# Sliding-window attention and a gated MLP: q and k loaded as four tokens per partition, and the first batch taken into the common loop

## The chip, the cores and the metric

The kernel runs on one core of a Trainium2 chip. The metric is device time in microseconds (us), the median of several executions. The core has five engines that run side by side and wait for one another through semaphores: TensorE (PE in the profile, with its weight loads as PEld), VectorE (DVE), ScalarE (ACT), GpSimd (POOL) and SyncE (SP). SP, ACT and POOL also start DMA transfers; SP does nothing else here. SBUF and PSUM are on-chip memories of 128 partitions; TensorE writes its results to PSUM.

## The reference

Eight batches, each with 8 heads, 576 tokens and 64 elements per head, all in float32. Attention looks back over a window of 64 tokens; the heads are then joined to 512 columns per token, and a gated MLP (gMLP) mixes along the tokens.

```python
scores = (q @ k.T) / sqrt(64)
mask = (rel >= 0) & (rel < 64)          # rel = query position - key position
attn = softmax(where(mask, scores, -1e9))
x = (attn @ v), heads joined            # 8 x 576 x 512

h = maximum(x @ w_in, 0)                # 512 -> 1024
u, v = h[..., :512], h[..., 512:]
v_n = (v - mean(v)) / sqrt(var(v) + 1e-6)
v_s = einsum('ts,bsd->btd', w_spatial, v_n) + b_spatial[None, :, None]
out = (u * v_s) @ w_out                 # 8 x 576 x 512
```

`w_spatial` is 576 x 576: it mixes all tokens of a batch, and `b_spatial` has one value per token.

## The kernel before

**Layout.** The 576 tokens of a batch are 512 plus 64: four chunks of 128 and a remainder. q, k and v come in as float32 (`NAT`, two sets of buffers, so batches i and i+2 share one), and are cast to float16 (`F16`, two sets). In the chunk layout partition p of chunk c holds token 128c + p, so every run of a load is one token of one head: 64 floats, 256 bytes. `hs` is a copy of v shifted by 64 tokens (`shift_pair`, `shift_half`), so that any 128 neighbouring keys that begin at a multiple of 64 stand in one tile.

**Attention of one batch, five steps.** Steps 0 to 3 each take two heads over the first 512 tokens, step 4 takes the remainder of all heads. `emit_T` transposes k and q of two heads on PE (eight transposes into one PSUM tile `tp`, of which there is one) and copies the tile to `qk` with one DVE copy (L216). `emit_S` multiplies each block of 64 keys with the 128 queries that may see it (16 small matmuls, into the one `sc`). `emit_E` takes the exponential on ACT and masks it with a minimum on DVE. `emit_P` computes the softmax's denominators (two matmuls with `onesK`) and the weighted sum of v (16 matmuls), into the one `oz`. `emit_N1` and `emit_N2` form the reciprocal as exp(-ln z) on ACT and multiply on DVE: the result X is a transposed x, float16.

**gMLP of one batch, units.** V (5 units; matmuls, ReLU on ACT, statistics on DVE), LN (two small ACT operations, five DVE operations that write `vn`), U (5), G (5; the spatial matmuls over `wspT`, then a DVE product) and O (5; matmuls with w_out, an ACT copy into `ob`, which has three buffers, and an output DMA). All matmul results of these units share three PSUM tiles (`mm`). `emit_W` transposes w_spatial on PE into `wspT` once; the bias lies in its row 64 of the last tile.

**Order.** Nothing is scheduled by a planner: every engine executes its instructions in the order in which the program writes them. A stage i of the main loop (from i = 2) interleaves the attention of batch i with V, LN, U, G of batch i-1 and O of batch i-2. In `att_step` the order within a step is: transposes of the next step, two units, S, P of the step before, then E, N1, N2 with one unit after each, then the units left. In stage i the loads of batch i+1 are issued on SP (L76), and POOL casts them in the same stage (L88). The kernel's last stages, 8 and 9, hold the gMLP of batch 7 and its O.

**The opening.** Batch 0 is loaded and attended pair by pair, two heads at a time: `load_by_pairs` issues 27 transfers, of which four of v are on ACT's queue and the others on SP's. `casts_step` casts k on ACT, q on DVE, v on POOL for one pair just before its transposes. Between these steps 51 matmuls on a zero tile (`warm`) run on PE. The weights are loaded and cast by DMAs that POOL issues after pairs 2 and 3 and after the remainder. Batch 1 is loaded on SP in the same pairwise form. When batch 0's attention is done, PE does V of batch 0, the five `emit_W`, LN and three U; then batch 1's attention follows with the rest of gMLP 0, its O included, between its steps (L486 to L489). The outputs of batches 0 and 1 go out on ACT's queue, the later ones on SP's (L407). Batch 2 is loaded by chunks on SP before batch 1's first transpose group is written.

Of the kernel before, what the change touches and what calls it, by code (L numbers as in the profile page):

```python
# [13 lines left out]
B = 8  # L14
# [5 lines left out]
def kernel(  # L20
# [44 lines left out]

    def load_heads(b, x, h0, eng):
        for h in (h0, h0 + 1):
            eng.dma_start(NAT[b][x][:, 0:4, h, :],  # L68
                          SRC[x][b, h, 0:512, :].rearrange("(c p) d -> p c d", p=128))
# [38 lines left out]
    scratch = cpool.tile([128, 512], f16, name="scratch")  # L108
    nc.vector.memset(scratch[:], 0.0)  # L109

    def warm(n):
        t = psp.tile([128, 512], f32, tag="mm", bufs=3, name=f"warm{nc.next_id()}")
        for _ in range(n):
            nc.tensor.matmul(t[:, :], scratch[:, 0:128], scratch[:, :], start=True, stop=True)  # L114

    def load_by_pairs(b):
        new_batch(b)
        for p in range(4):
            for x in (1, 0, 2):
                load_heads(b, x, 2 * p, nc.scalar if (b == 0 and p < 2 and x == 2) else nc.sync)  # L120
        for x in (1, 0, 2):
            load_rem(b, x, nc.sync)

    load_by_pairs(0)
    new_half(0)
    warm(16)
# [16 lines left out]
    mask = cpool.tile([128, 2, 8, 64], f16, name="mask")  # L143
    maskr = cpool.tile([128, 8, 64], f16, name="maskr")
    for h in (0, 1):
        for u in range(8):
            if u % 2 == 1:
                nc.vector.tensor_copy(mask[:, h, u, :], keep[:])
            else:
                nc.vector.tensor_scalar(mask[:, h, u, :], keep[:], -1.0, BIG, ALU.mult, ALU.add)  # L150
        nc.vector.memset(mask[64:128, h, 0, :], 0.0)
    for u in range(8):
        nc.vector.tensor_copy(maskr[:, u, :], mask[:, 0, 2, :])
# [8 lines left out]
    def casts_step(b, s, engk, engq):  # L162
        if s < 4:
            cast_pair(b, 1, s, engk)
            cast_pair(b, 0, s, engq)
            cast_pair(b, 2, s, nc.gpsimd)
            shift_pair(b, s, nc.gpsimd)
        else:
            for x in (1, 0, 2):
                cast_rem(b, x, nc.gpsimd)  # L170
            shift_rem(b, nc.gpsimd)

    class _Act:
        @staticmethod
        def tensor_copy(o, i):
            nc.scalar.copy(o, i)  # L176


    w_in_sb = [cpool.tile([128, 1024], f16, name=f"win{r}") for r in range(4)]
    w_out_sb = [cpool.tile([128, 512], f16, name=f"wout{r}") for r in range(4)]  # L180
# [383 lines left out]
```

## Time and profile before

| | |
|---|---|
| Time, median of 3 runs | 251.05 us (249.46 to 251.18) |
| The profiled execution's own time | 251.05 us |
| Its span, first to last instruction | 249.3 us |
| Mean granted TensorE clock | 0.962 |
| PE busy | 227.3 us, 91% |
| DVE busy | 155.3 us, 62% |
| ACT busy | 152.2 us, 61% |
| POOL busy | 122.1 us, 49% |
| DMA | 120,014 packets, 40.41 MB, 162 GB/s; 113,776 packets under 512 B |

A row of the profile names the source line, the engine, the operation, what it writes and reads with the number of partitions and elements, how often, its duration, and the idle time of the engine in front of it with what ended that. In rows in order of time the first number is the start in us from the span's start, the second the duration. In the slices a digit is the busy share of a fortieth of the span, in tenths. In a row of windows the columns are the stretch, its length, then the busy time of PE, PEld, DVE, ACT and POOL, the granted clock, the DMA engines' share (above 1 where queues overlap) and GB/s. Matmuls overlap in the pipeline, so the distance from one start to the next says more of PE than a duration does. The rows of a DMA queue give its packets, MB and the share of sixteen engines' span that its packets took: q1 is SP's queue, q10 ACT's, q0 POOL's.

### The profile page before, as it was taken

The page shows a single profiled execution, that of the slowest core. Times are in us where ns is not written, and L with a number is a line of the kernel's source. Part 1 is how long each engine was busy: PE and PEld are TensorE (multiplying, and loading weights), DVE is VectorE, ACT ScalarE, POOL GpSimd, SP SyncE. Part 2 cuts the span into 40 slices and gives each one's busy share as a digit, 9 for nine tenths or more (in the row PEclk, how much of TensorE's full clock was granted, in tenths as well). Part 3 has the DMA queues.
Part 4 walks back from the last instruction along what each step waited for, and adds up shares of the span by engine and source line. Part 5 has one row for each costly group of instructions (what it writes and reads, how often), then busy time and mean ns, then how long its engine had stood idle before and what let it go on. Part 6 is the DMA issues. An engine that isn't in the chain of part 4 may idle for free.

```text
span 249.3 us, 6391 instructions
## 1 busy us (share of the span) xinstructions
PE 227.3 (91%) x2588; PEld 116.8 (47%) x2588; DVE 155.3 (62%) x317; ACT 152.2 (61%) x266; POOL 122.1 (49%) x183
## 2 busy tenths in 40 slices
PE   7784996996399999999999999999999999999893
PEld 3442453553254464436544554455445544553351
DVE  6453277562459782887479556966597659755630
ACT  3373484446447666766785577756776677767423
POOL 3469638875499695369016592469135900000000
PEclk9999799799569999999999999999999999999998
DMA  8999999999999996992389948995499040014005
GB/s 159 218 184 208 216 204 229 191 201 276 249 199 210 198 178 175 246 206 52 128 192 211 192 128 221 189 198 135 137 216 156 27 165 5 3 42 149 0 3 189
DMA packets 120014, 40.41 MB, mean 162 GB/s; under 512 B 113776, under 2 KB 114864, under 8 KB 119984
## 3 DMA queue, kind: packets, MB, share of 16 engines
q1 hardware_dynamic: 114720, 34.88, 70.1%
q0 software_dynamic: 1840, 2.24, 5.2%
q10 hardware_dynamic: 3424, 2.88, 4.1%
q8 instruction: 20, 0.33, 0.6%
q14 instruction: 10, 0.08, 0.1%
HBM read 32.79 MB, written 9.44 MB: 169 GB/s over the span
## 4 chain that ended last, share of the span: by engine, by line
PE 60%; DVE 13%; ACT 9%; DMA 8%; SPq 3%; POOL 2%; issue 2%; ACTq 1%; POOLq 0%
SPq L68 3%; DMA nv_80<-in_v_dram 2%; DMA out_dram<-ob_0_1033 2%; DMA out_dram<-ob_1_3433 2%; DMA nq_78<-in_q_dram 2%; ACTq L407 1%; PE ps_0_804 L382 1%; PE warm_583 L114 1%; PE pv_0_1308 L330 1%; PE ps_0_4590 L382 1%; PE ps_0_4237 L382 1%; DVE mv_172 L336 1%; PE ps_0_3720 L382 1%; PE ps_1_895 L382 0%; PE ps_3_4653 L382 0%
## 5 line engine op out<-in xcount | busy, mean ns | idle before, releaser
L88 POOL CAST hq_2281<-nq_2285 128x512 f16<-128x512 f32 (+1 forms) x5 | 3.2, 635 | 12.8 <-DMA nq_2285<-in_q_dram 12.8
L114 PEld LDWEIGHTS <-scratch 128*128 128x128 f16 x51 | 5.0, 112 | 7.3 <-issue 3.8
L88 POOL CAST hq_3389<-nq_3393 128x512 f16<-128x512 f32 (+1 forms) x5 | 3.9, 797 | 8.8 <-DMA nq_3393<-in_q_dram 8.8
L281 PEld LDWEIGHTS <-onesK 128*64 128x64 f16 x80 | 4.6, 107 | 7.5 <-issue 5.2
L88 POOL CAST hq_2835<-nq_2839 128x512 f16<-128x512 f32 (+1 forms) x5 | 3.6, 720 | 8.3 <-DMA nq_2839<-in_q_dram 8.3
L176 ACT CAST hk_109<-nk_79 128x512 f16<-128x512 f32 x4 | 2.5, 618 | 7.5 <-DMA nk_79<-in_k_dram 7.5
L114 PE MATMUL warm_113<-scratch 128*128 128x512 f16 x16 | 5.5, 524 | 1.3 <-DVE scratch L109 1.3
L81 POOL CAST hv_110<-nv_80 128x512 f16<-128x512 f32 x4 | 2.5, 632 | 8.3 <-DMA nv_80<-in_v_dram 7.3
L88 POOL CAST hv_1729<-nv_1733 128x512 f16<-128x512 f32 (+1 forms) x5 | 3.5, 708 | 4.4 <-DMA nv_1733<-in_v_dram 4.4
L88 POOL CAST hq_1727<-nq_1731 128x512 f16<-128x512 f32 (+1 forms) x5 | 2.9, 609 | 4.6 <-DMA nq_1731<-in_q_dram 4.6
L88 POOL CAST hv_2283<-nv_2287 128x512 f16<-128x512 f32 (+1 forms) x5 | 3.2, 637 | 3.8 <-DMA nv_2287<-in_v_dram 3.8
L81 POOL CAST hv_433<-nv_437 128x512 f16<-128x512 f32 x4 | 2.5, 613 | 5.2 <-DMA nv_437<-in_v_dram 5.1
L88 POOL CAST hv_1184<-nv_764 128x512 f16<-128x512 f32 (+1 forms) x5 | 3.1, 611 | 3.9 <-DMA nv_764<-in_v_dram 3.9
L362 PEld LDWEIGHTS <-win_181 128*128 128x128 f16 x32 | 3.1, 98 | 3.8
L362 PEld LDWEIGHTS <-win_182 128*128 128x128 f16 x32 | 3.1, 98 | 3.8
L88 POOL CAST hv_1220<-nv_1224 128x512 f16<-128x512 f32 (+1 forms) x5 | 3.9, 780 | 2.0 <-DMA nv_1224<-in_v_dram 2.0
L88 POOL CAST hq_1182<-nq_762 128x512 f16<-128x512 f32 (+1 forms) x5 | 3.3, 654 | 3.2 <-DMA nq_762<-in_q_dram 2.7
L81 DVE CAST hq_108<-nq_78 128x512 f16<-128x512 f32 x4 | 1.7, 432 | 4.8 <-DMA nq_78<-in_q_dram 4.8
L281 PE MATMUL oz_3_1153<-e_1_3_1108,onesK 128*64 128x512 f16 x2 | 0.6, 611 | 4.4 <-DVE x_2_1133 L308 4.4
L88 POOL CAST hv_3391<-nv_3395 128x512 f16<-128x512 f32 (+1 forms) x5 | 3.0, 611 | 2.8 <-DMA nv_3395<-in_v_dram 2.8
L88 POOL CAST hv_2837<-nv_2841 128x512 f16<-128x512 f32 (+1 forms) x5 | 3.3, 666 | 2.0 <-DMA nv_2841<-in_v_dram 1.8
L264 ACT ACTIVATE e_1_0_831<-sc_0_813 128x1024 f16<-128x1024 f32 x1 | 1.0, 1023 | 5.2 <-PE sc_0_813 L242 5.2
(1871 smaller groups left out, 940.3 us busy)
## 6 DMA issues: line engine op xcount, KB each, us to landing
nk_79<-in_k_dram SPq DMA_DIRECT2D x9, 128.0 KB, 3.9
nq_78<-in_q_dram SPq DMA_DIRECT2D x9, 128.0 KB, 4.1
nk_436<-in_k_dram SPq DMA_DIRECT2D x9, 128.0 KB, 4.8
nq_435<-in_q_dram SPq DMA_DIRECT2D x9, 128.0 KB, 4.8
nv_437<-in_v_dram SPq DMA_DIRECT2D x9, 128.0 KB, 4.1
nk_763<-in_k_dram SPq DMA_DIRECT2D x4, 256.0 KB, 5.5
nq_762<-in_q_dram SPq DMA_DIRECT2D x4, 256.0 KB, 5.7
nv_764<-in_v_dram SPq DMA_DIRECT2D x4, 256.0 KB, 6.0
```

What stands on the lines that cost most here:

```text
L68: eng.dma_start(NAT[b][x][:, 0:4, h, :], SRC[x][b, h, 0:512, :].rearrange("(c p) d -> p c d", p=128))
L81: eng.tensor_copy(F16[b][x][:, 0:4, hs, :], NAT[b][x][:, 0:4, hs, :])
L88: eng.tensor_copy(F16[b][x][0:sn, c, :, :], NAT[b][x][0:sn, c, :, :])
L114: nc.tensor.matmul(t[:, :], scratch[:, 0:128], scratch[:, :], start=True, stop=True)
L176: nc.scalar.copy(o, i)
L264: nc.scalar.activation(e2[:, :, :], sc[:, :, :], AF.Exp, bias=0.0, scale=0.125)
L281: nc.tensor.matmul(oz[64 * h:64 * h + 64, 1, 0:n], onesK[:, :], e2[:, h, 0:n], start=True, stop=True)
L330: nc.tensor.matmul(pv[0:jn, :], xcol(b, r, j), w_in_sb[r][:, 512:1024], start=(r == 0), stop=(r == 3))
L336: nc.vector.bn_aggr(mv_t[b % NSB][0:jn, j, :], st6[0:jn, 0:6])
L362: nc.tensor.matmul(pu[:, :], w_in_sb[r][:, 128 * m:128 * m + 128], X[b, r][:, :], start=(r == 0), stop=(r == 3))
L382: nc.tensor.matmul(ps[:, :], VN[b, kk][0:kn, 128 * m:128 * m + 128], wspT[kk][0:kn, 0:512], start=(kk == 0), stop=(kk == 4))
L407: (nc.scalar if b < 2 else nc.sync).dma_start(out[b, 128 * j:128 * j + jn, :], ob[0:jn, :])
```

## The change

q and k of the first 512 tokens are loaded in another order: partition p holds tokens 4p to 4p+3 of a head, which lie side by side in memory, so a run is 1 KB (`load_pairs4`). v and the remainders stay in 256-byte runs. `cast_pair4` casts one head at a time into the old shape of `F16`, whose chunk index is now j, the token's place among the four. After the transposes column 128j + p of q and k stands for token 4p + j. Keys are put back in token order when the k half of `tp` is copied to `qk`; queries stay in the new order through S, the mask, P, X and the whole gMLP. Therefore S and P address the queries of a block as four runs (32 or 16 columns each), w_spatial is loaded and transposed in the same order, the bias row is reordered by an ACT copy, and each output DMA writes rows 4p + j.

The special opening goes. Batch 0's loads stay pairwise, now with all of v on ACT's queue; its k is cast on POOL, its q on DVE, all in front of the loop; the warm matmuls go. All weight DMAs stand on POOL after batch 0's casts and before batch 1's. The common loop now starts at i = 0: stage 0 is attention 0 with the five W at its end, stage 1 attention 1 with V, LN, U, G of batch 0, stage 2 has O of batch 0. The loads of batch i+2 are written in stage i (in stage 0 those of batches 1 and 2), three per step, in front of the step's units; the casts of batch i+1 stay in stage i. All outputs go on SP's queue.

```diff
+    def load_pairs4(b, x, h0, n, eng):
+        eng.dma_start(NAT[b][x][:, 0:4, :, :].rearrange("p j h d -> p (j h d)")
+                      .rearrange("p (h e) -> p h e", h=8)[:, h0:h0 + n, :],
+                      SRC[x][b, h0:h0 + n, 0:512, :].rearrange("h (p j) d -> p h (j d)", j=4))
+    def cast_pair4(b, x, p, eng):
+        src = NAT[b][x][:, 0:4, :, :].rearrange("p j h d -> p (j h d)") \
+            .rearrange("p (h j d) -> p h j d", h=8, j=4)
+        for h in (2 * p, 2 * p + 1):
+            eng.tensor_copy(F16[b][x][:, 0:4, h, :], src[:, h, :, :])
...
-    load_by_pairs(0)
+    new_batch(0)
     new_half(0)
-    warm(16)
+    for p in range(4):
+        for x in (1, 0):
+            load_pairs4(0, x, 2 * p, 2, nc.sync)
+        load_heads(0, 2, 2 * p, nc.scalar)
+    for x in (1, 0, 2):
+        load_rem(0, x, nc.sync if x != 2 else nc.scalar)
...
+    for p in range(4):
+        cast_pair4(0, 1, p, nc.gpsimd)
+        cast_pair4(0, 0, p, nc.vector)
+        cast_pair(0, 2, p, nc.gpsimd)
+        shift_pair(0, p, nc.gpsimd)
+    for x in (1, 0, 2):
+        cast_rem(0, x, nc.gpsimd)
+    shift_rem(0, nc.gpsimd)
...
+        nc.gpsimd.dma_start(t[:], moe_w_in[128 * r:128 * (r + 1), :])
+    nc.gpsimd.dma_start(wq[:], moe_w_spatial[0:512, :].rearrange("(p j) s -> p j s", j=4))
+    nc.gpsimd.dma_start(wr[:], moe_w_spatial[512:576, :])
+    nc.gpsimd.dma_start(brow[64:65, :], moe_b_spatial[:].unsqueeze(0))
+        nc.gpsimd.dma_start(t[:], moe_w_out[128 * r:128 * (r + 1), :])
...
-                nc.vector.tensor_copy(qk[:, :], tp[:, :])
+                nc.vector.tensor_copy(qk[:, 512:1024].rearrange("d (p j) -> d p j", j=4),
+                                      tp[:, 512:1024].rearrange("d (j p) -> d p j", j=4))
+                nc.vector.tensor_copy(qk[:, 0:512], tp[:, 0:512])
...
-                        nc.tensor.matmul(sc[r:r + 64, h, c0:c1],
-                                         qk[d, 512 + 64 * kap:576 + 64 * kap], qk[d, c0:c1],
+                        nc.tensor.matmul(sc[r:r + 64, h, :].rearrange("k (j p) -> k j p", j=4)[:, :, p0:p1],
+                                         qk[d, 512 + 64 * kap:576 + 64 * kap], q4[d, :, p0:p1],
                                          start=True, stop=True)
...
+                    if s < 4:
+                        o_ = o_.rearrange("k (j p) -> k j p", j=4)[:, :, 16 * u:16 * u + 16]
+                        e_ = e_.rearrange("k (j p) -> k j p", j=4)[:, :, 16 * u:16 * u + 16]
...
-        (nc.scalar if b < 2 else nc.sync).dma_start(out[b, 128 * j:128 * j + jn, :], ob[0:jn, :])
+        dst = out[b, 0:512, :].rearrange("(p j) d -> p j d", j=4)[:, j, :] if j < 4 else out[b, 512:576, :]
+        nc.sync.dma_start(dst, ob[0:jn, :])
...
         nc.scalar.copy(wspT[kk][0:sn, 0:576], wps[0:sn, 0:576])
+        if kk == 4:
+            nc.scalar.copy(wspT[4][64:65, 0:512].rearrange("r (j p) -> r j p", j=4),
+                           brow[64:65, 0:512].rearrange("r (p j) -> r j p", j=4))
+            nc.scalar.copy(wspT[4][64:65, 512:576], brow[64:65, 512:576])
...
+    def load_list(b):
+        fs = []
+        for x in (1, 0):
+            def first(x=x):
+                if b not in NAT:
+                    new_batch(b)
+                load_pairs4(b, x, 0, 4, nc.sync)
+            fs += [first, lambda x=x: load_pairs4(b, x, 4, 4, nc.sync),
+                   lambda x=x: load_rem(b, x, nc.sync)]
+        return fs + [lambda c=c: load_chunk(b, 2, c) for c in range(5)]
...
+    emit_T(0, 0)
+    for i in range(B + 2):
+        st = units(i)
...
+        if i == 0:
+            new_batch(1)
+            loads += load_list(1)
+        if i + 2 < B:
+            loads += load_list(i + 2)
         if i + 1 < B:
             new_half(i + 1)
-            for x in (1, 0, 2):
-                casts += [lambda x=x, c=c: cast_chunk(i + 1, x, c, nc.gpsimd) for c in range(5)]
+            for x in (1, 0):
+                casts += [lambda x=x, p=p: cast_pair4(i + 1, x, p, nc.gpsimd) for p in range(4)]
+                casts += [lambda x=x: cast_rem(i + 1, x, nc.gpsimd)]
+            casts += [lambda c=c: cast_chunk(i + 1, 2, c, nc.gpsimd) for c in range(5)]
             casts += [lambda hf=hf: shift_half(i + 1, hf, nc.gpsimd) for hf in range(3)]
+        nl = (len(loads) + 4) // 5
+        ncst = (len(casts) + 3) // 4
...
-                nxt = None
-            if i < B or s == 0:
-                att_step(i, s, st[s], 2, 1, nxt)
-            run_units(st[s], 99)
+                emit_T(*nxt)
+            for _ in range(2 if i else 0):
+                if todo:
+                    todo.pop(0)()
...
```

`units(i)` returns the unit lists of a stage as the old loop wrote them (O of i-2 in step 0, V of i-1 in step 1, LN, U and G in steps 2 to 4), and in stage 0 the five W in step 4. The order within a step is that of `att_step`.

## The prediction

> **What bounds the kernel now.** I read the page's slices first, then 2 us windows for the DMA rate, then ACT, PE, DVE and POOL in order of time.
>
> ```profile
> PE   7784996996399999999999999999999999999893
> PEclk9999799799569999999999999999999999999998
> DMA  8999999999999996992389948995499040014005
> ```
>
> A slice is 6.2 us. From 69 us on PE is full, from 75 us its clock is whole: the middle and the end are bound by TensorE. Before that the DMA engines are full and PE has holes, the largest in the slice at 62 us. So a change to loading and to the first batches is priced before 92 us; from there only what lengthens or shortens a TensorE-bound stage counts.
>
> The start of T(i,1), the second transpose group of stage i, marks the stages:
>
> ```profile
> 92.10 0.39 PE L210 MATMUL tp_1_1744<-id_130,hk_1219 128*128 128x128 f16 x4
> ...
> 118.28 0.39 PE L210 MATMUL tp_1_2298<-id_130,hk_1728 128*128 128x128 f16 x4
> ```
>
> Stage 3 begins at 92.1, stage 4 at 118.3, stage 5 at 144.4: 26.1 us each. Stages 3 to 9 have the same unit order in both kernels. If the new stage 2, whose units are also those of stages 3 to 7 (O, V, LN, U, G), has its T(2,1) at t, the end is 249.3 - (92.1 - 26.1) + t = **t + 183.3**, but for what the stages themselves gain or lose. All of the question is t.
>
> The hole at 62 us shows the mechanism to watch (ACT, then PE, in order of time):
>
> ```profile
> 55.58 0.39 ACTq L407 DMA_DIRECT2D out_dram<-ob_0_1033  x1
> ...
> 60.55 0.58 ACT L406 COPY ob_3_1117<-po_3_1111 128x512 f32<-128x512 f32 x1 [0.92 <-DMA out_dram<-ob_0_1033]
> ```
> ```profile
> 64.64 0.64 PE L281 MATMUL oz_3_1153<-e_1_3_1108,onesK 128*64 128x512 f16 x2 [4.36 <-DVE x_2_1133 L308]
> ```
>
> ob has three buffers, so ob_3 waits until the output of ob_0 has landed (4.9 us among the loads, 2.0 when the queue is empty); ACT is held, and PE loses 4.4 us behind it. That was on ACT's own DMA queue.
>
> **Part 1, the DMA stream.** In pure 256-byte loads the rate is flat:
>
> ```profile
> 4.00:6.00 2.00, 2.00 (x9) 0.75 (x6) 1.66 (x12) 0.62 (x1) 0.65 (x2) 1.00 1.39 218
> 6.00:8.00 2.00, 1.43 (x12) 0.73 (x10) 0.61 (x3) 0.00 (x0) 1.18 (x2) 1.00 1.39 218
> ```
>
> 218 GB/s is 16 x 256 B / 218 = 18.8 ns per packet and engine. A batch is 13,824 such packets (3.54 MB), 16.2 us. After the change q and k are 2,048 packets of 1 KB, with 1,024 of 256 B for the remainders and 4,608 for v. No load here has 1 KB runs. Its price lies between 18.8 ns (a packet costs the same) and 75 ns (four times the bytes). From the queue rows
>
> ```profile
> q1 hardware_dynamic: 114720, 34.88, 70.1%
> q0 software_dynamic: 1840, 2.24, 5.2%
> q10 hardware_dynamic: 3424, 2.88, 4.1%
> ```
>
> q10 is 2,048 v packets and 1,376 of about 1.7 KB: 85 ns each in busy time, where q1's small ones take 22.9. A line through the two gives 55 ns for 1 KB, and scaled by 18.8/22.9 about 48 ns, which I take. A batch is then (2,048 x 48 + 5,632 x 18.8)/16 = **12.8 us**, 3.4 less.
>
> The Trainium skill ("DMA: Bandwidth & Descriptors", Specifications) gives about 27 GiB/s per engine and line rate from 512 B up, so 35 ns for 1 KB as an estimate; a batch would be 11.1 us, the first output below some 8 us earlier, and the sum 245.6.
>
> The loads also move. Before, batch 2 was issued from 44.6 us on; now SP holds batches 1 and 2 in stage 0, batch 3 in stage 1 and k of batch 4 at the head of stage 2, all ahead of the five outputs of batch 0, which change from ACT's queue to SP's. SP runs ahead as far as buffers allow: the casts that free batch 1's and 2's inputs are over early (below), so the stream never pauses, and the first output stands at its end: 2 (first bytes) + 4 x 12.8 + weights 10.3 (2.24 MB at 218) + k of batch 4 3.7 = 67 us. The same sum for the kernel before (2 + 3 x 16.2 + 10.3 + 5.4 of outputs = 66.3) stands against a last landing of batch 2 at 68.4, so I add 6% for pauses: 71, and 2.0 for landing: **73 us**. With the packet's two bounds: 55 to 89.
>
> **Part 2, the opening on POOL and PE.** The casts of k of batch 0 go from ACT to POOL, all its q casts stand ahead of the first qk copy on DVE (q of pair 3 lands after eight 256 KB transfers of 0.77 us and seven of v of 0.60, at 12.3, so attention starts at about 13 us, not 8), ACT issues nine v loads ahead of its first exponential (four took 3.13 us, so 7 us, over by then), the 51 warm matmuls go, and gMLP 0 moves from between batches 0 and 1 into stage 1. POOL now decides, since T(1,0) stands on PE ahead of S(0,4) and waits for k and q of batch 1:
>
> ```profile
> 68.41 0.61 POOL L88 CAST hv_1184<-nv_764 64x512 f16<-64x512 f32 x1 [0.43 <-DMA nv_764<-in_v_dram]
> 68.97 1.03 POOL L103 COPY hs_1185<-hv_1184 64x1024 f16<-64x1024 f16 x1
> 70.06 1.04 POOL L104 COPY hs_1185<-hv_1184 64x1024 f16<-64x1024 f16 x1
> ```
>
> 512 elements take 0.61, 1,024 take 1.04; POOL has no 256-element cast. Between 0.31 (half) and 0.61 I take 0.40, from its 128-element select (0.29). Batch 0: four pairs of 2 x 0.40 + 0.61 + 2 x 0.65 and gaps, 2.75 each from 4.5 us on, and 2.4 of remainders, 17.9; or 20.3 if v of pair 3 lands at 16. I take 19.5. Then eleven weight DMAs at 0.55, of which the last three wait for w_in to land (4.5 to 6.7 us after issue): 8, to 27.5. Then k and q of batch 1, 16 x 0.40 + 2 x 0.6 = 7.6, to 35.1; T(1,0) can start at 32. v 3.1 and four shifts 4.2: P(1,0) at **42.4** (38 to 48). ACT's chain over wspT and the two new bias copies (5.4 us from T(1,0)) ends before that. In the kernel before, P(2,0) at 74.5 to T(3,1) at 92.1 is the same work, 17.6 us; with 1.0 for a low clock after the idle opening (0.5 and 0.6 in the slices at 62 to 75 us, after the hole) t = **61.0**. Without anything else the end is 244.3.
>
> **Part 3, the stages.** k's evacuation splits from one 1,024-element copy (0.65 to 0.69) into a strided and a plain one. The plain half is qkr's row (0.40 to 0.42). A strided PSUM read is in no row: 0.42 if stride is free, 1.38 if it halves the rate of x_0's row (0.67, one element at a time); I take 0.69. Follow-on spacing makes it +0.35 per copy. Only the one in front of the five vn is near the path:
>
> ```profile
> 132.19 0.65 DVE L216 COPY qk_3_2538<-tp_3_2528 128x1024 f16<-128x1024 f16 x1
> 132.88 0.41 DVE L352 TENSOR_SCALAR vn_0_2544<-vs_0_2422,mv_172,rs_2541 128x512 f16<-128x512 f16 x1
> ...
> 133.53 0.70 DVE L352 TENSOR_SCALAR vn_2_2548<-vs_2_2485,mv_172,rs_2541 128x512 f16<-128x512 f16 x1
> ...
> 134.47 0.69 DVE L352 TENSOR_SCALAR vn_1_174<-vs_4_2513,mv_172,rs_2541 64x512 f16<-64x512 f16 x1
> ```
>
> The two long vn stand beside POOL casts. In the new kernel inputs lie ready a stage earlier and POOL's casts fall around the stage boundary, so the vn may all run at 0.33 spacing: -0.4 against +0.35. I take -0.5 in all (-3 to +7). The other copies have 0.5 us or more of DVE idleness behind them.
>
> S and P now read and write PSUM and SBUF in four runs of 16 or 32. No row has that. The 16 matmuls of S advance PE by 0.34 us and those of P by 0.35, about 22 ns each, where S streams up to 128 columns and P 64, so they seem bound by issue: I take nothing; doubled they cost 4 x 0.69 = 2.8 a stage, 19 over seven. [...]
>
> **The sum.** Profiled run: span 249.3, time 251.05 (1.75 around it), which is also the median. Opening -5.0 (66.0 to 61.0), stages -0.5: 243.8. At t = 61.0 ob_3 would be ready at 66.0 (4.96 after T, as 118.28 to 123.24); it waits for 73: +7.0, and 0.5 of clock: 251.3, time **253.0**. The 5 us won are given back at the first outputs, and 2 more.
>
> **Rivals.**
> - *The stream is ahead of the outputs* (1 KB packets below about 37 ns, or the weights' 10.3 us mostly beside the loads; it decides where output 0 lands before 66 us): 243.8 + 1.75 = 245.6. For it: 319 GB/s between 60 and 62 us where outputs mix in. Against: DMA shares of 9 tenths for 90 us.
> - *1 KB runs bring nothing*, the change doesn't do what it says: output 0 at 89, 269. Against: the queue rows.
> - *Strided matmuls cost double*, on PE in every stage from 1 on: 253 + 19 = 272. It decides from some 0.14 us per group, which over 56 groups is 8 us, more than the opening wins. For it: no row has such an access. Against: their issue-bound spacing.
>
> **Chances.** Outputs held (249 to 258) 0.47; stream ahead 0.29; packets no cheaper 0.12; strided matmuls 0.12. 80% range: 245 to 268, from the first rival to just short of the other two. One per cent is about what can be told from no change here. Faster 0.29, within 0.21 (the lower half of the forecast), slower 0.50.
>
> **What would show it.** Right: ob_3 of batch 0 waiting for the output of ob_0 for some 7 us near 70 us, a 12 to 13 us batch, PE idle from about 22 to 32 waiting for POOL, later stages near 26. Wrong: no wait at ob_3; P(1,0) away from 42; S or P groups above 0.4 us; a strided copy above 0.8.

## The result, and the profile after

The changed kernel takes **262.54 us** (median of four runs, 261.34 to 263.52). The kernel before, timed on the same chip, takes 250.25 us (249.06 to 251.18). The ratio is **1.049** (95% interval 1.041 to 1.057): slower by 4.9%, where 253.0 us was forecast. The profiled execution took 261.34 us with a span of 259.5 us, so 1.84 us lie around the span, against 1.75 before. The spans differ by 10.2 us.

The slices of the page (one is 6.5 us) and the row of SP's queue:

```profile
PE   0047149968989999999899989998999999999893
PEclk9999999997999999999999999999999999999999
DMA  7999998999877962697169805960500040005005
...
q1 hardware_dynamic: 63472, 36.58, 56.1%
```

The 1 KB runs do what they say: SP's queue moves 36.58 MB (it has all outputs now) in 63,472 packets and 56.1% of the engines' time, against 34.88 MB in 114,720 packets and 70.1%. The DMA engines are full to about 58 us, not to 90. Yet PE starts later (the digits up to 32 us are 0, 0, 4, 7, 1), and it no longer fills its slices afterwards.

PE in order of time (start, duration, then the idle time in brackets with what ended it):

```profile
33.03 0.61 PE L205 MATMUL tp_0_496<-id_102,hk_227 128*128 128x128 f16 x4 [6.27 <-POOL hk_227 L76]
36.33 0.61 PE L208 MATMUL tp_0_496<-id_102,hq_226 128*128 128x128 f16 x4 [2.69 <-POOL hq_226 L76]
...
47.99 0.42 PE L240 MATMUL sc_1_711<-qk_1_622 64*64 64x128 f16 x16
48.34 0.41 PE L279 MATMUL oz_0_729<-e_1_0_655,onesK 128*64 128x512 f16 x2
...
71.25 0.39 PE L205 MATMUL tp_1_1129<-id_102,hk_594 128*128 128x128 f16 x4
...
99.10 0.39 PE L205 MATMUL tp_1_1691<-id_102,hk_1111 128*128 128x128 f16 x4
...
126.07 0.39 PE L205 MATMUL tp_1_2253<-id_102,hk_1673 128*128 128x128 f16 x4
...
142.95 0.29 PE L216 MATMUL tp_4_2590<-id_102,hk_1673 64*128 64x64 f16 x4
...
151.84 0.41 PE L279 MATMUL oz_3_2743<-e_4_3_2657,onesK 128*64 128x512 f16 x2 [1.20 <-DVE x_2_2693 L311]
...
153.04 0.39 PE L205 MATMUL tp_1_2815<-id_102,hk_2235 128*128 128x128 f16 x4
```

The stage marks T(2,1), T(3,1), T(4,1), T(5,1) stand at 71.25, 99.10, 126.07 and 153.04. Against the aligned 66.0, 92.10, 118.28 and 144.36 of the kernel before that is 5.3, 7.0, 7.8 and 8.7 us late, and 10.2 at the end. So half of the loss is there before stage 2, and the stages add the rest: 27.8 us from the first of these marks to the second and 27.0 between the next ones, instead of 26.1. The line at 151.84 shows where in a stage: PE stands still in front of P(4,3). Its counterpart in the kernel before follows S(4,4) without a wait:

```profile
143.16 0.41 PE L281 MATMUL oz_3_2782<-e_4_3_2697,onesK 128*64 128x512 f16 x2
```

What it waits for is seen on DVE and POOL in that same stage 4 of the changed kernel:

```profile
145.44 0.69 DVE L388 TENSOR_TENSOR g_1_2617<-ps_1_2610,ru_1_2561 128x512 f16<-128x512 f32 x1 [0.73 <-PE ps_1_2610 L385]
146.86 3.72 DVE L268 TENSOR_TENSOR e_4_3_2657<-e_4_3_2657,mask 128x1024 f16<-128x1024 f16 x1 [0.72 <-ACT e_4_3_2657 L262]
...
151.11 0.68 DVE L311 TENSOR_TENSOR x_2_2693<-oz_2_2637,zi_2_2691 128x512 f16<-128x512 f32 x1
```
```profile
143.36 2.80 POOL L76 CAST hk_2797<-nk_2239 128x256 f16<-128x256 f32 x8 [8.78 <-issue]
146.12 0.61 POOL L96 CAST hk_2797<-nk_2239 64x512 f16<-64x512 f32 x1
146.68 2.81 POOL L76 CAST hq_2796<-nq_2238 128x256 f16<-128x256 f32 x8
149.43 0.61 POOL L96 CAST hq_2796<-nq_2238 64x512 f16<-64x512 f32 x1
```

The minimum that masks e of step 3 takes **3.72 us**; in the kernel before the same one took 0.69:

```profile
139.45 0.69 DVE L270 TENSOR_TENSOR e_4_3_2697<-e_4_3_2697,mask 128x1024 f16<-128x1024 f16 x1 [0.73 <-ACT e_4_3_2697 L264]
```

The long one ends at 150.58, half a microsecond after POOL's last q cast (150.04). POOL's inputs lie ready two batches ahead, so its casts of batch 6 start the moment T(4,4) (at 142.95) has read the buffer for the last time, and run 0.345 us apart without a gap for 6.7 us. The minima of step 3 in stages 2 to 5 all take 3.72 us. Behind them stand g_2 and x_2, and x_2 must free oz before P(i,3) may write it. The products from PSUM (g_1 at 145.44, 0.69 us) pass beside the same casts unhindered.

In stage 1 POOL is busy for 28.1 of 29.4 us (windows: stretch, length, busy time of PE, PEld, DVE, ACT, POOL, clock, DMA share, GB/s), and there too long instructions stand on DVE:

```profile
41.90:71.25 29.35, 25.68 (x295) 13.40 (x295) 23.24 (x38) 16.38 (x30) 28.11 (x53) 0.94 1.08 244
```
```profile
49.64 3.37 DVE L268 TENSOR_TENSOR e_1_1_749<-e_1_1_749,mask 128x1024 f16<-128x1024 f16 x1
...
66.35 2.24 DVE L268 TENSOR_TENSOR e_1_3_971<-e_1_3_971,mask 128x1024 f16<-128x1024 f16 x1 [0.73 <-ACT e_1_3_971 L262]
...
71.23 2.53 DVE L268 TENSOR_TENSOR e2r_1077<-e2r_1077,maskr 128x512 f16<-128x512 f16 x1
```

And the wait that the forecast put at 7 us is not there (SP, then ACT, in order of time):

```profile
73.37 0.36 SPq L411 DMA_DIRECT2D out_dram<-ob_0_1148  x1
```
```profile
77.09 0.58 ACT L409 COPY ob_3_1210<-po_3_1204 128x512 f32<-128x512 f32 x1
```

SP issues the first output of batch 0 right behind its copy (72.76 and 0.58), and ob_3 has no idle time in front of it.

### The profile page after: what moved, and what is told of

Read it like the earlier page. It is cut to its first block, busy times and chain, and to the rows that moved or that the text cites. A ratio compares the mean times of both kernels' runs of the same rounds, so it can differ in the third digit from the quotient of the medians.

```text
span 259.5 us, 6319 instructions
## 1 busy us (share of the span) xinstructions
PE 219.3 (85%) x2537; PEld 115.2 (44%) x2537; DVE 182.4 (70%) x352; ACT 150.8 (58%) x264; POOL 125.5 (48%) x240
## 3 DMA queue, kind: packets, MB, share of 16 engines
q1 hardware_dynamic: 63472, 36.58, 56.1%
## 4 chain that ended last, share of the span: by engine, by line
PE 54%; DVE 22%; DMA 10%; ACT 6%; POOL 4%; issue 2%; ACTq 0%
DMA nv_78<-in_v_dram 4%; DMA win_187<-in_moe_w_in_dram 4%; DVE e_5_3_3219 L268 1%; DVE e_4_3_2657 L268 1%; DVE e_2_3_1533 L268 1%; DVE e_3_3_2095 L268 1%; DVE e_1_1_749 L268 1%; DMA nk_77<-in_k_dram 1%; POOL hk_227 L76 1%; DMA out_dram<-ob_1_4667 1%; DVE e_1_3_971 L268 1%; PE ps_1_924 L385 1%; PE pu_2_916 L365 1%; PE pv_0_689 L333 1%; PE ps_0_4203 L385 1%
## 5 line engine op out<-in xcount | busy, mean ns | idle before, releaser
L279 PEld LDWEIGHTS <-onesK 128*64 128x64 f16 x80 | 5.3, 109 | 11.5 <-issue 8.9
L205 PEld LDWEIGHTS <-hk_80 128*128 128x128 f16 x16 | 1.4, 129 | 13.8 <-POOL hk_80 L76 13.0
L205 PE MATMUL tp_1_244<-id_102,hk_80 128*128 128x128 f16 x4 | 0.6, 302 | 7.8 <-DVE qk_0_220 L213 7.8
L76 POOL CAST hk_1673<-nk_1115 128x256 f16<-128x256 f32 x8 | 2.8, 394 | 8.8 <-issue 8.8
L76 POOL CAST hk_2235<-nk_1677 128x256 f16<-128x256 f32 x8 | 2.8, 394 | 8.8 <-issue 8.8
L76 POOL CAST hk_2797<-nk_2239 128x256 f16<-128x256 f32 x8 | 2.8, 394 | 8.8 <-issue 8.8
L76 POOL CAST hk_3359<-nk_2801 128x256 f16<-128x256 f32 x8 | 2.8, 394 | 8.8 <-issue 8.8
L211 DVE COPY qk_0_506<-tp_0_496 128x512 f16<-128x512 f16 x1 | 0.7, 692 | 8.2 <-PE tp_0_496 L208 8.2
L76 DVE CAST hq_79<-nq_76 128x256 f16<-128x256 f32 x8 | 2.9, 402 | 5.0 <-DMA nq_76<-in_q_dram 5.0
L266 ACT ACTIVATE e2r_547<-sc_4_509 128x512 f16<-128x512 f32 x1 | 0.6, 597 | 9.3 <-PE sc_4_509 L254 9.3
L205 PE MATMUL tp_0_496<-id_102,hk_227 128*128 128x128 f16 x4 | 0.6, 307 | 6.3 <-POOL hk_227 L76 6.3
L365 PEld LDWEIGHTS <-win_187 128*128 128x128 f16 x32 | 3.2, 99 | 3.9 <-issue 0.3
L365 PEld LDWEIGHTS <-win_189 128*128 128x128 f16 x32 | 3.2, 99 | 3.9 <-issue 0.3
L205 PE MATMUL tp_0_210<-id_102,hk_80 128*128 128x128 f16 x4 | 0.6, 308 | 4.9 <-POOL hk_80 L76 4.9
L205 PEld LDWEIGHTS <-hk_227 128*128 128x128 f16 x16 | 1.3, 122 | 7.0 <-POOL hk_227 L76 6.4
L76 POOL CAST hk_80<-nk_77 128x256 f16<-128x256 f32 x8 | 3.3, 435 | 2.2 <-DMA nk_77<-in_k_dram 2.0
L100 POOL CAST hv_3360<-nv_2802 128x512 f16<-128x512 f32 (+1 forms) x5 | 3.0, 648 | 2.5 <-PE oz_3_3305 L294 2.5
L100 POOL CAST hv_1674<-nv_1116 128x512 f16<-128x512 f32 (+1 forms) x5 | 3.0, 648 | 2.5 <-PE oz_3_1619 L294 2.5
L100 POOL CAST hv_2236<-nv_1678 128x512 f16<-128x512 f32 (+1 forms) x5 | 3.0, 648 | 2.5 <-PE oz_3_2181 L294 2.5
L100 POOL CAST hv_2798<-nv_2240 128x512 f16<-128x512 f32 (+1 forms) x5 | 3.0, 648 | 2.5 <-PE oz_3_2743 L294 2.5
L268 DVE TENSOR_TENSOR e_2_3_1533<-e_2_3_1533,mask 128x1024 f16<-128x1024 f16 x1 | 3.7, 3723 | 0.7 <-ACT e_2_3_1533 L262 0.7
## 6 DMA issues: line engine op xcount, KB each, us to landing
nk_77<-in_k_dram SPq DMA_DIRECT2D x4, 256.0 KB, 5.1
nq_76<-in_q_dram SPq DMA_DIRECT2D x4, 256.0 KB, 5.5
nv_225<-in_v_dram SPq DMA_DIRECT2D x4, 256.0 KB, 17.3
```

The costliest lines, as they stand in the source:

```text
L76: eng.tensor_copy(F16[b][x][:, 0:4, h, :], src[:, h, :, :])
L100: eng.tensor_copy(F16[b][x][0:sn, c, :, :], NAT[b][x][0:sn, c, :, :])
L205: nc.tensor.transpose(tp[:, 512 + 128 * c:640 + 128 * c], Kh[:, c, 2 * s:2 * s + 2, :], id16[:, :])
L211: nc.vector.tensor_copy(qk[:, 512:1024].rearrange("d (p j) -> d p j", j=4), tp[:, 512:1024].rearrange("d (j p) -> d p j", j=4))
L266: nc.scalar.activation(e2[:, :, :], sc[:, :, 0:256], AF.Exp, bias=0.0, scale=0.125)
L268: nc.vector.tensor_tensor(e2[:, :, :], e2[:, :, :], m, ALU.min)
```

## The experiments

**Theories.** A: POOL's unbroken rows of casts keep DVE's minima waiting, and P with them. Its two forms: any row does it (A1), or only rows of 256-element casts (A2). B: the strided copies and matmuls lengthen the stages. C: the loss is in the opening. And from the prediction: the outputs are held.

All kernels in one table. The third column is the start of x of step 3 of batch 1 on DVE (a mark that is easy to find in each trace), then the distance to the same mark of batch 2, and the distances after that up to batch 5. Each row is from that kernel's own profiled execution; the times are medians, the ratio is to the kernel before, timed beside each.

| kernel | time, ratio (95%) | mark | stage 2 | later |
|---|---|---|---|---|
| before | 250.25 | 67.0 | 25.9 | 26.2, 26.1, 26.1 |
| after | 262.54, 1.049 (1.041 to 1.057) | 74.0 | 26.3 | 27.0, 27.0, 27.0 |
| e1 POOL waits for the minimum | 259.64, 1.037 (1.032 to 1.042) | 76.5 | 25.7 | 25.7, 25.7, 25.7 |
| e2 plain copy | 262.23, 1.046 (1.037 to 1.056) | 74.3 | 26.8 | 26.8, 26.8, 26.8 |
| e3 layout alone | 261.70, 1.043 (1.036 to 1.050) | 72.7 | 27.7 | 26.2, 27.0, 27.8 |
| e4 order alone | 266.43, 1.064 (1.058 to 1.070) | 72.2 | 36.9 | 25.5, 25.5, 25.5 |
| e5 casts of 512 | 254.31, 1.013 (1.009 to 1.018) | 66.9 | 30.0 | 25.7, 25.7, 25.7 |
| e6 layout alone, casts of 512 | 258.42, 1.030 (1.026 to 1.034) | 72.2 | 25.8 | 25.8, 28.0, 25.5 |
| e7 order alone, ACT outputs | 263.80, 1.050 (1.045 to 1.055) | 72.5 | 26.4 | 27.3, 32.7, 25.5 |
| e8 casts of 512, opening by pairs | 254.88, 1.016 (1.011 to 1.022) | 61.9 | 36.8 | 25.7, 25.7, 25.7 |
| e9 as e8, ACT outputs | 250.09, 0.996 (0.993 to 1.000) | | | |
| e10 casts of 512, ACT outputs | 253.91, 1.014 (1.007 to 1.020) | 71.0 | 24.6 | 27.3, 25.7, 25.7 |
| e11 casts of 256 by tokens | 264.23, 1.055 (1.050 to 1.059) | 75.1 | 27.0 | 27.0, 27.0, 27.0 |
| e12 as e8, six ob buffers | **246.26, 0.982 (0.977 to 0.986)** | 62.1 | 25.9 | 25.7, 25.7, 25.7 |

(No marks are given for e9, whose profiled execution, 252.29 us, is the longest of its ten.)

### e1: POOL waits for the minimum

```diff
+    def pool_gap(b):
+        nc.gpsimd.tensor_copy(gapt[:, :], LASTMIN[b][0:1, 0, 0:1])   # the masked e2 of step 3
...
             for x in (1, 0):
+                if x == 0 and i > 0:
+                    casts.append(lambda i=i: pool_gap(i - 1))
                 casts += [lambda x=x, p=p: cast_pair4(i + 1, x, p, nc.gpsimd) for p in range(4)]
```

> The changed kernel with one more POOL instruction per stage: before the q casts of batch i+1 POOL copies one element of the masked e2 of step 3 of batch i-1, so it stands still until that minimum is through; nothing is left out. Theory A (POOL's unbroken row of casts, which begins when T(i,4) gives the buffer free, keeps the DVE minimum of step 3 waiting: 3.72 us against 0.69, and P of step 3 with it): the minimum of step 3 takes at most 1.2 us in stages 2 to 6, the 1.2 us PE wait in front of P(i,3) goes, stages of 27.0 become 25.3 to 26.0, and the time is 253 to 258. Theory B (strided copies and matmuls lengthen the stages): no change, 261 to 263.5. Theory C (all of the loss is in the opening and stage 1): at most 2 us less, stages still 27.0.

DVE, then POOL, in the stage at 148 us:

```profile
147.91 0.69 DVE L274 TENSOR_TENSOR e<-e,mask 128x1024 f16<-128x1024 f16 x1 [0.72 <-ACT e L268]
```
```profile
148.67 0.18 POOL L262 COPY gapt<-e 1x1 f16<-1x1 f16 x1 [0.89 <-DVE e L274]
```

With POOL standing still for 0.9 us the minimum takes 0.69 and all stages are 25.7, below the 26.1 of the kernel before. That part of A is shown: the casts, not DVE's own work, made the minimum long. B falls for the stages, as the strided copies and matmuls are all still there. The time fell by 2.9 us only, less than A expected (253 to 258 us), because stage 1 grew:

```profile
56.87 7.32 DVE L363 TENSOR_SCALAR vn<-vs,mv,rs 128x512 f16<-128x512 f16 x5
```

In stage 1, where POOL has no idle time to give, the five vn took 7.3 us beside POOL's v casts and shifts (1.7 us in a later stage, where they start 0.32 us apart). The first of them alone took 3.4 us, over a row of five casts of 512 elements. PE, left without work, ran at a granted clock of 0.5 from 58 to 69 us.

### e2: the plain copy

```diff
-                nc.vector.tensor_copy(qk[:, 512:1024].rearrange("d (p j) -> d p j", j=4),
-                                      tp[:, 512:1024].rearrange("d (j p) -> d p j", j=4))
-                nc.vector.tensor_copy(qk[:, 0:512], tp[:, 0:512])
+                nc.vector.tensor_copy(qk[:, :], tp[:, :])
```

> The changed kernel with one plain copy of 1024 columns from tp to qk as before, in place of the strided and the plain copy of 512; the keys stay in the loaded order, so the order of the keys is left out and the output is not the reference's. Theory A: DVE gets 0.41 us per step back, but the minimum of step 3 still waits for the end of POOL's row of casts (about 3.5 us): 259 to 262. Theory B: the four copies are the price of a stage, 27.0 becomes 25.5 to 26 and the time 254 to 257. Theory C: 260 to 262.

e2 leaves out the return of the keys to token order. It takes 262.23 us against 262.54, with overlapping intervals. A stage is 0.2 us shorter, and its minimum of step 3 still takes 3.72. The reordering at evacuation costs nothing that this measurement can tell.

### e3 and e4: each half of the change alone

e3 is the kernel before with the new layout. The core of its diff is the loads, the rest is as in the change:

```diff
-                load_heads(b, x, 2 * p, nc.scalar if (b == 0 and p < 2 and x == 2) else nc.sync)
+                if x == 2:
+                    load_heads(b, x, 2 * p, nc.scalar if (b == 0 and p < 2) else nc.sync)
+                else:
+                    load_pairs4(b, x, 2 * p, 2, nc.sync)
...
-            loads = [(i + 1, x, c) for x in (1, 0, 2) for c in range(5)]
+            loads = load_list(i + 1)
...
```

> The layout alone: the opening, the order and the loads' distance (batch i+1 in stage i) of the kernel before, with four tokens per partition in loads, casts, S, mask, P, w_spatial and outputs as in the changed kernel. Theory A: casts are paced by the loads that land in the same stage, so no minimum waits over 1.5 us from stage 3 on, stages stay at 26 or below, and the 1 KB packets take some us off the first 90: 243 to 250. Theory B: stages of 27, 254 to 258. Theory C: the loss is gone with the opening, 245 to 251.

e4 is the changed kernel with the old layout; of its diff the loads of batch 0 and the casts are shown, and mask, copy, S, P, w_spatial and outputs go back in the same way:

```diff
-            load_pairs4(0, x, 2 * p, 2, nc.sync)
+            load_heads(0, x, 2 * p, nc.sync)
...
-                casts += [lambda x=x, p=p: cast_pair4(i + 1, x, p, nc.gpsimd) for p in range(4)]
-                casts += [lambda x=x: cast_rem(i + 1, x, nc.gpsimd)]
+                casts += [lambda x=x, c=c: cast_chunk(i + 1, x, c, nc.gpsimd) for c in range(5)]
...
```

> The order alone: the changed kernel's opening, common loop, loads two batches ahead and outputs on SP, with the chunk layout, 256-byte runs, 512-element chunk casts, one copy to qk and contiguous S and P as before. Theory A: once the loads are a stage ahead the casts of k and q run without a gap from T(i,4) on and a minimum of step 3 takes over 2 us in the stages from 4 on; opening as in the changed kernel or later by the slower packets: 258 to 266. Theory B: stages of 26 or below throughout, 250 to 257. Theory C: T(2,1) at 71 or later, stages near 26, 256 to 262.

Either half alone is as bad as both, and for different reasons. In e3 minima of 2.8 and 2.6 us stand in batch 1's stage and of 3.7, 3.2 and 3.9 later, against the expectation that paced loads would leave none over 1.5. So a load distance of one batch does not protect DVE: C's 245 to 251 falls, and A's own 243 to 250 with it.

e4 has no minimum over 1.3 us, although its casts of 512 elements also run in a row from T(i,4) on (this is what set A2 against A1), and its stages are 25.5. But here the forecast wait appears, on ACT at ob_3 of batch 0:

```profile
87.54 0.59 ACT L400 COPY ob<-po 128x512 f32<-128x512 f32 x1 [11.54 <-DMA out_dram<-ob]
```

With 256-byte runs the first output has landed at 87.5 us.

### e5 and e11: what in the casts does it

```diff
-        for h in (2 * p, 2 * p + 1):
-            eng.tensor_copy(F16[b][x][:, 0:4, h, :], src[:, h, :, :])
+        hs = slice(2 * p, 2 * p + 2)
+        eng.tensor_copy(F16[b][x][:, 0:4, hs, :], src[:, hs, :, :].rearrange("p h j d -> p j h d"))
```

> The changed kernel with one POOL (for batch 0's q DVE) cast of 512 elements for two heads in place of two of 256; the same values go to the same places. Theory A2 (it is the form: rows of 256-element casts, 0.345 us apart and 0.394 long, keep a minimum waiting to the end of the row, rows of 512-element casts don't, since with the order alone the minimum in front of such a row took 1.03 us): the minimum of step 3 takes at most 1.1 us, stages 25.5 to 26, no minimum over 1.5 us in stage 1 either, 253 to 257. Theory A1 (any row without a gap does it, whatever its form): the minimum of step 3 takes 3 us or more, stages 26.7 to 27, 260 to 262.5. Theory C (opening and stage 1 alone): 260 to 262.

e11 keeps 256 elements and cuts them another way:

```diff
-        for h in (2 * p, 2 * p + 1):
-            eng.tensor_copy(F16[b][x][:, 0:4, h, :], src[:, h, :, :])
+        hs = slice(2 * p, 2 * p + 2)
+        for j in (0, 2):
+            eng.tensor_copy(F16[b][x][:, j:j + 2, hs, :],
+                            src[:, hs, j:j + 2, :].rearrange("p h j d -> p j h d"))
```

> The changed kernel with its casts of q and k still at 256 elements and as many, but cut by two tokens of two heads in place of four tokens of one head, so that what is written stands in runs of 128 elements and not of 64. If the number of elements of a cast (its 0.345 us) lets the row starve DVE: the minimum of step 3 takes 3 us or more, stages 26.7 to 27, 260 to 263. If the pattern of the access does: the minimum takes at most 1.1 us, stages 25.7, 253.5 to 257.

e5, POOL, DVE and ACT:

```profile
141.84 2.77 POOL L76 CAST hq<-nq 128x512 f16<-128x512 f32 x4
```
```profile
142.54 1.03 DVE L268 TENSOR_TENSOR e<-e,mask 128x1024 f16<-128x1024 f16 x1 [0.72 <-ACT e L262]
```
```profile
75.41 0.58 ACT L409 COPY ob<-po 128x512 f32<-128x512 f32 x1 [4.40 <-DMA out_dram<-ob]
```

e11, POOL and DVE:

```profile
148.44 2.81 POOL L77 CAST hq<-nq 128x256 f16<-128x256 f32 x8
```
```profile
148.63 3.72 DVE L270 TENSOR_TENSOR e<-e,mask 128x1024 f16<-128x1024 f16 x1 [0.73 <-ACT e L264]
```

This one edit takes **8.2 us** off the changed kernel. In e5 the minimum begins inside a row as before, but gets in within 0.34 us: POOL's four q casts take 2.77 instead of 2.28, so POOL gave way. In e11, with other runs but still 256 elements, it waits for the end of the row, 3.72 as in the changed kernel, and the time is 264. So it is the number of elements of a cast, not its pattern. The moment at which a minimum arrives doesn't explain it either: casts of 256 held minima that began between 0.03 and 0.31 us after the start of a cast, over three casts and more (27 of 30 in the traces of these kernels), and casts of 512 let most of those in that began in the same span. A2 holds, with a limit: rows of 512 can also hold a minimum, as this one of e10 shows, in stage 1 where POOL's rows follow one another:

```profile
67.60 3.14 DVE L268 TENSOR_TENSOR e2r<-e2r,maskr 128x512 f16<-128x512 f16 x1
```

e8 has one of 3.2 and e6 two of 3.3 and 2.9. Which of them gets in was not settled. It adds to the spread of stage 1: e5 and e10 are the same up to batch 0's first output, and their marks are 66.9 and 71.0. Of these 4.1 us, 2.2 come with the minimum shown; the other 1.9 stood before it, where e10's granted clock was 0.72 and 0.85 (56 to 60 us and 60 to 64 us) and e5's 1.00.

The line of ACT shows the price of being earlier: T(2,1) of e5 is at 66.1, and now ob_3 waits 4.4 us. In the changed kernel, with T(2,1) at 71.25, there was no such wait.

### e6: the layout alone, with casts of 512

The edit of e5 in e3.

> The layout alone, as in the run of that name, and the 512-element casts for two heads in it. Theory A2: no minimum over 1.5 us, the multiplication by pairs in batch 1's stage loses no time against the kernel before, stages 25.5 to 26, so the time is 247 to 252. Theory A1: minima of 2 us and more remain where POOL's casts stand close, 258 to 262.

258.42, 3.3 us below e3, not 10 to 15. As written down this is A1's outcome: the time lies in its 258 to 262, and two minima stay long, 3.3 us in batch 1's stage and 2.9 in the stage of 28.0 us. So casts of 512 do not always let a minimum in, and in the old order the layout may lose for another reason too. ACT in batch 1's stage:

```profile
57.67 0.57 ACT L430 COPY ob<-po 128x512 f32<-128x512 f32 x1
59.69 0.36 ACTq L432 DMA_DIRECT2D out_dram<-ob  x1
60.09 0.58 ACT L430 COPY ob<-po 128x512 f32<-128x512 f32 x1 [1.85 <-DMA nk<-in_k_dram]
61.92 0.41 ACTq L432 DMA_DIRECT2D out_dram<-ob  x1
```

Between the end of a copy (58.24, 60.67) and the issue of its output lie 1.45 and 1.25 us, and 1.9 at the fourth; in the kernel before they came 0.03 to 0.04 us behind. The trace names loads as what ended the wait. How much of the loss is this and how much the two minima was not tested.

### e7: the order alone, with ACT's queue for the first outputs

```diff
-        nc.sync.dma_start(out[b, 128 * j:128 * j + jn, :], ob[0:jn, :])
+        (nc.scalar if b < 2 else nc.sync).dma_start(out[b, 128 * j:128 * j + jn, :], ob[0:jn, :])
```

> The order alone, with the outputs of batches 0 and 1 on ACT's queue as in the kernel before. In the order alone ob_3 of batch 0 waited 11.5 us for an output that stood behind 256-byte loads on SP, the step that the prediction put at 7 us for the changed kernel, where it did not show. If that wait is the queue's: ACT waits under 3 us at ob_3 of batch 0, the stage of 36.9 becomes 25.5 to 28, and the time 255 to 259. If the loads hold the DMA engines whatever the queue: the wait stays over 8 us, 263 to 267.

ob_3 of batch 0 waits no more, and stage 2 is 26.4. But the time is 263.80, and the stage of 32.7 shows why:

```profile
137.23 0.58 ACT L400 COPY ob<-po 128x512 f32<-128x512 f32 x1 [7.97 <-DMA out_dram<-ob]
```

Batch 2 is the first whose outputs stand on SP, and it meets the same wait. Neither case that was written down is quite right: the wait is that of SP's queue, but as long as SP is behind with 256-byte loads it only moves to the next output there.

### e8: the opening by pairs

e8 is e5 with batch 1 loaded and cast pair by pair; the four w_out transfers (`load_wout`) move behind batch 1's casts.

```diff
-            loads += load_list(1)
+            for p in range(4):
+                loads += [lambda x=x, p=p: load_pairs4(1, x, 2 * p, 2, nc.sync) for x in (1, 0)]
+                loads += [lambda p=p: load_heads(1, 2, 2 * p, nc.sync)]
...
+        if i == 0:
+            casts = []
+            for p in range(4):
+                casts += [lambda x=x, p=p: cast_pair4(1, x, p, nc.gpsimd) for x in (1, 0)]
+                casts += [lambda p=p: cast_pair(1, 2, p, nc.gpsimd), lambda p=p: shift_pair(1, p, nc.gpsimd)]
+            casts += [lambda x=x: cast_rem(1, x, nc.gpsimd) for x in (1, 0, 2)]
+            casts += [lambda: shift_rem(1, nc.gpsimd), load_wout]
```

> The changed kernel with 512-element casts for two heads and two edits to the opening: batch 1 is loaded and cast pair by pair (k, q, v, shift) as in the kernel before, and the four w_out transfers are issued on POOL after batch 1's casts, not in front of them. Theory C (V, W, LN and U of batch 0 come late because POOL and the load of v hold T(1,0) to 33 to 36 us and P(1,0) to 48.3 us): T(1,0) at 25 to 28, P(1,0) at 39 to 44, and 4 to 8 us less than the run with the 512-element casts alone. If the weights' landing (wq 13.5 us after its issue) bounds stage 0: 0 to 3 us less.

PE, SP and ACT in order of time:

```profile
24.86 0.61 PE L207 MATMUL tp<-id,hk 128*128 128x128 f16 x4
...
43.55 0.41 PE L281 MATMUL oz<-e,onesK 128*64 128x512 f16 x2
...
61.15 0.39 PE L207 MATMUL tp<-id,hk 128*128 128x128 f16 x4
```
```profile
69.63 1.59 SPq L413 DMA_DIRECT2D out_dram<-ob  x3
```
```profile
75.99 0.58 ACT L411 COPY ob<-po 128x512 f32<-128x512 f32 x1 [9.92 <-DMA out_dram<-ob]
```

T(1,0) at 24.9, P(1,0) at 43.6 and T(2,1) at 61.2: C is right on the marks, 5 us ahead of e5. Nothing of it is left in the time (254.88 against 254.31). SP reaches the outputs at 69.6, behind loads, 6.4 us after the first of them was ready (ob_0's copy ends at 63.2). It lands at 76.0, another 6.4 us later, and ob_3 waits 9.9 us where it waited 4.4.

### e9, e10 and e12: the held outputs

e9 is e8, and e10 is e5, with the outputs of batches 0 and 1 on ACT's queue (the edit of e7). e12 is e8 with:

```diff
-        vs = mpool.tile([128, 512], f16, tag=f"vs{j}", bufs=2, name=f"vs{b}_{j}")
+        vs = mpool.tile([128, 512], f16, tag=f"vs{j}", bufs=1, name=f"vs{b}_{j}")
...
-        ob = mpool.tile([128, 512], f32, tag="ob", bufs=3, name=f"ob{b}_{j}")
+        ob = mpool.tile([128, 512], f32, tag="ob", bufs=6, name=f"ob{b}_{j}")
```

> The changed kernel with 512-element casts for two heads, batch 1 loaded and cast by pairs, w_out after its casts, and the outputs of batches 0 and 1 on ACT's queue as in the kernel before. The run without the last edit reached the x of batch 1's step 3 at 61.9 us, 5 us ahead of the kernel before, and then waited 9.9 us at ob_3 of batch 0 for an output that SP issued at 69.6, behind loads. If the order on SP's queue is what holds the outputs: ACT waits under 2 us there, no later stage is over 27 us, and the time is 244 to 248, faster than the kernel before. If the stream of loads holds whatever is sent: the wait at ob_3 stays above 6 us, or a later stage waits as long for its loads, and the time is 251 to 255.

> The changed kernel with 512-element casts for two heads and the outputs of batches 0 and 1 on ACT's queue, opening as in the changed kernel. In the run with the casts alone ob_3 of batch 0 waited 4.4 us. If the queue's order is the cause: that wait under 1 us, the stage of 29.97 becomes 25.7 to 26.5, 249.5 to 251.5. If the stream is: 253 to 255.

> The changed kernel with 512-element casts for two heads, batch 1 loaded and cast by pairs, w_out after its casts, all outputs still on SP, but six ob buffers in place of three, for which the ReLU results of V have one buffer per chunk in place of two. If what the late outputs cost is the wait for an ob buffer: no wait of ACT for an output of batch 0, the stage of 36.8 in the run with three buffers becomes 25.7 to 27, and the time is 245 to 250, at or ahead of the kernel before and of the run with ACT's queue (250.1). If the loads behind the late outputs then come late: a stage after the second takes over 28 us, 251 to 255.

e9: 250.09, 4.8 us below e8, but not 244 to 248. Why it falls short is open; in its profiled execution, the longest of ten, ob_3 still waits 1.6 us. e10: the wait at ob_3 is gone (its copy at 74.44 follows without one), but stage 1 was 4.1 us longer in that execution, and the times spread from 252.5 to 256.0; nothing is to be told from it but the wait. e12 is the clean one, with ACT's first and fourth copy of batch 0 3.4 us apart and SP as late as before:

```profile
68.72 0.84 SPq L413 DMA_DIRECT2D out_dram<-ob  x1
```
```profile
66.22 0.59 ACT L411 COPY ob<-po 128x512 f32<-128x512 f32 x1
```

No wait, stage 2 of 25.9, 246.26 us, inside the 245 to 250 that were expected. What the late outputs cost was the wait for a buffer of ob; here the outputs still came late, and no later stage was longer than 25.7. This version beats both kernels: 1.8% below the kernel before, 6% below the changed one.

## Why the prediction was right and wrong

The side was right (slower) and 262.5 lies inside the range of 245 to 268, but the forecast mechanism was absent from the changed kernel, and the time came from two losses that its sum did not have: that the side was right is luck. By its own sum: 243.8 for a span with t = 61.0 and stages at -0.5, plus 7.5 for the held outputs and clock, is 251.3. Measured: T(2,1) at 71.25 is **+10.25**; from there to the end 188.25 instead of 182.8 is **+5.45**; the held outputs and their clock are **-7.5**. Together +8.2, the 259.5 of the span.

- **Stages, -0.5 (-3 to +7): failed.** The step was "POOL's casts fall around the stage boundary, so the vn may all run at 0.33 spacing". The vn do run at 0.32. But POOL's row starts where T(i,4) frees the buffer, in the middle of step 3, and what it meets is a minimum, and the stages are 27.0 us, not near 26. I had priced contention for vn alone, since the trace of before has its long ones there; the minima of 1.13 and 1.32 us at 113.4 and 87.2 us in that same trace, each beside POOL's copies, were the warning (the second is shown below). e1 and e5 settle it: 25.7 without the wait.
- **Opening, t = 61.0: failed by 10.25,** in two terms. P(1,0) came at 48.3, not 42.4. The eleven weight DMAs took 12 us on POOL (20.2 to 32.2) instead of 8, since w_in landed 8.3 to 11 us after its issue and not 4.5 to 6.7 (POOL waited 4.23, 0.87 and 0.99 us for it; the first wait is shown below), and then v of batch 1 was awaited for 1.8 us. From P(1,0) to T(2,1) it took 22.9, not 18.6: the starved minima and vn of stage 1. e5 takes T(2,1) to 66.1 by the casts alone, e8 to 61.2.
- **Held outputs, +7.0: absent here, and real.** The forecast had the first output landing at 73 us, with 89 for packets that are no cheaper. Landed: 75.4 in e5, 76.0 in e8, and 87.5 with 256-byte runs in e4. So these times were right within 3 us, in part by luck: in e8 SP issued the first output at 69.6, not 71, and it took 6.4 us to land, not 2.0. The sum has two slips besides: 55 ns scaled by 18.8/22.9 is 45, not 48, and 68.4 against 66.3 is 3%, not 6%. With both put right it would have given a landing at about 69.4 us, a wait of 3.4, and a time near 249.5, which is not slower. In the changed kernel PE came 10 us too late to meet any wait. In e8, where it comes at 61.2 as forecast, the wait is 9.9 and the time 254.9; that is the kernel nearest to the one forecast.
- **"The stream is ahead of the outputs" (245.6):** ob_3 did not wait in the changed kernel, as this rival had it, but its time did not come, since it kept t at 61; the first output landed after 66, not before.
- **"1 KB runs bring nothing" (269):** refuted, by 87.5 against 76.
- **"Strided matmuls cost double" (272):** refuted. S(1,1) at 47.99 and the group behind it at 48.34 are 0.35 apart, against 0.34 before. The page "PSUM — Partial Sum Buffer" of the Trainium skill (Specifications), by which any non-contiguous pattern slows matmuls significantly, does not hold for these matmuls in runs of 16 and 32, some 22 ns each: the measurement decides.
- **The strided copy, 0.69:** measured 0.68, and e2 finds no time in it.

A minimum beside one of POOL's copies in the kernel before, and POOL's first wait for w_in in the changed kernel:

```profile
87.19 1.32 DVE L270 TENSOR_TENSOR e_2_3_1589<-e_2_3_1589,mask 128x1024 f16<-128x1024 f16 x1 [0.73 <-ACT e_2_3_1589 L264]
```
```profile
86.94 1.03 POOL L103 COPY hs_1221<-hv_1220 64x1024 f16<-64x1024 f16 x1
```
```profile
28.78 0.54 POOL L190 DMA_DIRECT2D wout_204<-in_moe_w_out_dram  x1 [4.23 <-DMA win_183<-in_moe_w_in_dram]
```

The skill's page "SBUF — State Buffer" (Who interferes with whom) bears on the failed step, and I had not weighed it: a DVE instruction with two SBUF inputs contends with a GpSimd instruction that reads SBUF, the loser blocks wholly, and an instruction with at most one SBUF input does not contend, outside the two-port performance modes. The trace agrees: 3.72 us for the minimum, 0.69 for g_1 beside such casts. The five vn of e1, with one tensor input each, took 7.3 us beside POOL's work; in which mode they ran no run here shows. The page speaks of one instruction; here the loser waited not for one cast of 0.39 us but for the end of the row.

## What to carry to other kernels

Prefetching deeper does not only bring data earlier: it turns another engine's paced work into an unbroken row that starts when a buffer comes free, so look for what else runs at that moment, and for shared paths that the trace of the slower kernel shows only as a few instructions of odd length. Where VectorE works beside GpSimd, try few large GpSimd instructions in place of many small ones (here casts of 512 elements for 256: 8.2 us), and look again: rows of 512 still held some minima, and in e1 the vn. When a gain at the front disappears, look for a buffer of the output that waits behind loads on the same queue; three more buffers were worth 8.6 us here.

## What the runs showed of the hardware

- A VectorE minimum of two SBUF operands waits for a whole row of GpSimd casts of 256 elements (3.72 us for 0.69, in all twelve minima of step 3 in stages 2 to 5 of the changed kernel, e2 and e11), while in rows of 512 it mostly gets in at the next boundary (1.03 us) and sometimes doesn't (2.9 to 3.3 us in e6, e8 and e10). Who wins at a boundary was not settled.
- Five VectorE tensor_scalar operations on float16 took 7.3 us beside GpSimd's casts and copies (e1, stage 1), 1.7 in its later stages.
- Three of the first five output DMAs on ACT's queue were issued 1.2 to 1.9 us behind their copies while loads with 1 KB runs stood on SP's queue (e6), 0.03 to 0.04 us behind in the kernel before.
